# A new order for an attention turn, an identity matrix by VectorE, and tile addresses at multiples of 64 bytes, in a kernel of attention and two MLPs

## The chip, the cores and the metric

The kernel runs on one core of a Trainium2 chip. Its engines are TensorE (PE in the rows), VectorE (DVE), ScalarE (ACT), GpSimd (POOL) and SyncE (SP), which here issues nearly all loads and stores. Each engine works through its own queue in order and waits on semaphores for the others. The metric is the device time of one execution in microseconds (us), lower is better; the times given are medians of several runs.

## The reference

Linear attention with a feature map, then two MLPs, all in float32:

```python
def phi(x):                                   # q, k: (4, 8, 576, 64), w_phi: (64, 128)
    proj = np.einsum('bhsd,df->bhsf', x, w_phi)
    proj = proj - np.max(np.abs(proj), axis=-1, keepdims=True)
    return np.concatenate([np.exp(proj), np.exp(-proj)], axis=-1)
q_p, k_p = phi(q), phi(k)
kv = np.einsum('bhsf,bhsd->bhfd', k_p, v)
z = np.sum(k_p, axis=2)
x = np.einsum('bhsf,bhfd->bhsd', q_p, kv) / (np.einsum('bhsf,bhf->bhs', q_p, z)[..., None] + 1e-6)
x = x.transpose(0, 2, 1, 3).reshape(2304, 512)
h = x @ w1_in;  x = np.maximum(0.01 * h, h) @ w1_out          # w_in: (512, 2048), w_out: (2048, 512)
h = x @ w2_in;  out = (h * np.tanh(np.log1p(np.exp(h)))) @ w2_out   # h above 20: h itself
```

The MLP weights are random doubles; q, k, v and w_phi are float32.

## The kernel before

The 32 heads are worked in 16 pairs. A head has 576 positions: 512 main ones and 64 left over; the left-overs of two neighbouring pairs share a tile ("l" tiles, done every second turn). Products that need float32 accuracy are split in a high and a low half (`split`: ScalarE makes the high half, VectorE the low one) and done in three passes (`three`, L80 to L83). The products with kv and the second ones with q (`kv`, `nd`) are plain float32; each such matmul stands as two passes in the trace.

`attention(n)`, L435, is one turn. Three pairs are in work in it: t = n + 2 is loaded and transposed (`transposes`, L255, `q_left`, L282), p = n + 1 is projected (`q_proj` L316, `k_proj` L294, `k_proj_left` L304) and gets its exponentials of k (`k_exp` L402), w = n gets kv (L337) and the numerators and denominators (`nd` L355). The x of pair w - 1 is transposed into X (`x_t` L390). The order in which `attention` calls these is the order on every engine's queue: nothing reorders it later.

Some of what a turn does on the other engines: `q_proj` has ScalarE copy each of four pieces to qd, and after two of them GpSimd takes the maximum over partitions (`partition_all_reduce`, qm, L330; one for each head); `q_guard` (L333) subtracts it on VectorE. `k_guard` (L288) is a maximum and a subtraction on VectorE for each k projection. kv adds up in one PSUM bank, which ScalarE copies to the tile kv (L353); nd reads that tile. Banks come from two rings of four, "a" (projections, transposes) and "b" (kv, nd, x). The third `nd` of a pair (c == 2, the left-overs) keeps its bank as `lb` until `x_t` of the next turn has used it and VectorE has copied the result to X (L399).

Beside that the MLP weights, which come as pairs of 32-bit words of a double, are turned into float32: `Conv.step` (L121) takes one chunk of 128 x 512 in each turn from n = 1 on. VectorE clamps the high words (L147) and shifts the low ones (L149), ScalarE rebases (L150), VectorE puts sign and low bits together (e, L156) and, a turn later, joins them (c, L128); then the chunk is split (L166, L167) or stored to DRAM. `Conv.load` has SP load the next chunks into two `stage` buffers. After four of the turns, 8 to 11, `window` splits a part of X for the first MLP; turns 14 and 15 do the first two products of that MLP (`moe`) in place of transposes.

`load(i)` (L218) issues the loads of a pair on SP: kn, qn, for every second pair kl and ql, then the values vm and vl. The values have three buffers, so those of pair n + 3 go where those of pair n are. At the start `make_identity` (L194) has GpSimd build the identity that all transposes need; `start` (L407) works pairs 0 and 1 up to the first turn.

The functions that the diff touches, with their line numbers:

## Time and profile before

| what | value |
|---|---|
| median of 3 runs | 1033.09 us (1032.63 to 1036.21) |
| the profiled execution | 1029.51 us, span 1027.7 us |
| granted TensorE clock, mean | 0.999 |
| TensorE busy | 1001.1 us (97% of the span) |
| VectorE busy | 753.2 us (73%) |
| ScalarE busy | 501.3 us (49%) |
| GpSimd busy | 72.6 us (7%) |

A row of the timeline gives the start, the time, engine and line, operation, tiles (out<-in), shapes and count; in brackets the idle time of the engine before it and what ended that. Rows of one line that follow each other are put together, with their count behind an x. A row of the chain of waits gives the start, the time and the work that the end of the program hung on at that moment. The kernel's attention ends at about 241 us of the span; the rest is the two MLPs.

### The profile page before, as it was taken

To read this page: it belongs to the slowest core of one execution; us is meant where nothing else is said; L and a number is where in the kernel's file an instruction comes from. 1 tells how busy PE (TensorE), PEld (TensorE's weight loads), DVE (VectorE), ACT (ScalarE), POOL (GpSimd) and SP (SyncE) were. 2 spreads that over 40 slices of the span, in tenths; PEclk is the share of its full clock that TensorE was granted. 3 is DMA by queue.
4 is the path that set the end of the run, shared out by engine and by line. 5 is a ranking of instruction groups with operands and counts; after the bars stand their busy time and mean duration, and the time that the engine had idled before them with its cause. 6 is when DMAs were issued, how large, how long until landed. Compare 5 with 4: busy or idle time off the path is not lost.

```text
span 1027.7 us, 14556 instructions
## 1 busy us (share of the span) xinstructions
PE 1001.1 (97%) x5544; PEld 871.2 (85%) x5544; DVE 753.2 (73%) x1389; ACT 501.3 (49%) x839; POOL 72.6 (7%) x38
## 2 busy tenths in 40 slices
PE   6999999999999999999999999999999999999998
PEld 5999988998888888998888888888888988888886
DVE  5888898876995666666533546978876888868976
ACT  4666666654554333343333445545544555545543
POOL 3322333220000000000000000000000000000000
PEclk9999999999999999999999999999999999999999
DMA  4333323313541344444311221000100100001001
GB/s 130 111 111 111 100 82 93 121 43 113 160 148 42 123 144 154 134 144 136 110 62 31 93 82 62 1 1 0 41 1 1 41 1 21 1 1 41 1 1 42
DMA packets 55494, 72.84 MB, mean 71 GB/s; under 512 B 10496, under 2 KB 39808, under 8 KB 55424
## 3 DMA queue, kind: packets, MB, share of 16 engines
q1 hardware_dynamic: 55264, 71.84, 21.6%
q8 instruction: 44, 0.72, 0.3%
q14 instruction: 26, 0.21, 0.1%
q10 hardware_dynamic: 160, 0.07, 0.0%
HBM read 57.48 MB, written 14.42 MB: 70 GB/s over the span
## 4 chain that ended last, share of the span: by engine, by line
PE 92%; DVE 5%; issue 1%; ACT 1%; POOL 0%; ACTq 0%; DVEq 0%; POOLq 0%
PE a L81 14%; PE a L82 14%; PE a L83 14%; PE b L82 13%; PE b L81 13%; PE b L83 13%; PE b L373 6%; PE b L345 4%; DVE qd L335 1%; PE a L266 1%; DVE kd L291 1%; DVE mx L290 1%; ACT kv L353 1%; PE b L395 1%; PE b L350 1%
## 5 line engine op out<-in xcount | busy, mean ns | idle before, releaser
L81 PE MATMUL a<-wh,wh 128*128 128x512 f32 (+1 forms) x640 | 235.6, 368 | 0.0
L82 PE MATMUL a<-wl,wh 128*128 128x512 f32 (+1 forms) x640 | 235.4, 368 | 0.0
L83 PE MATMUL a<-wh,wl 128*128 128x512 f32 (+1 forms) x640 | 235.4, 368 | 0.0
L81 PEld LDWEIGHTS a<-wh,wh 128*128 128x128 f32 x640 | 120.6, 188 | 20.2
L82 PEld LDWEIGHTS a<-wl,wh 128*128 128x128 f32 x640 | 120.7, 189 | 20.1
L83 PEld LDWEIGHTS a<-wh,wl 128*128 128x128 f32 x640 | 120.6, 188 | 20.0
L571 DVE TENSOR_TENSOR gl<-g,gh 128x512 fp32r<-128x512 f32 x72 | 49.9, 693 | 110.1 <-ACT gh L568 110.1
L82 PE MATMUL b<-gl,wh 128*128 128x512 f32 (+1 forms) x320 | 117.7, 368 | 0.0
L81 PE MATMUL b<-gh,wh 128*128 128x512 f32 (+1 forms) x320 | 117.7, 368 | 0.0
L83 PE MATMUL b<-gh,wl 128*128 128x512 f32 (+1 forms) x320 | 117.7, 368 | 0.0
L82 PE MATMUL b<-wl,gh 128*128 128x512 f32 x288 | 112.1, 389 | 0.0
L81 PE MATMUL b<-wh,gh 128*128 128x512 f32 x288 | 112.1, 389 | 0.0
L83 PE MATMUL b<-wh,gl 128*128 128x512 f32 x288 | 112.1, 389 | 0.0
L568 ACT ACTIVATE gh<-g 128x512 fp32r<-128x512 f32 x72 | 45.5, 632 | 115.9 <-PE b L83 109.4
L330 POOL PARTITION_ALL_REDUCE qm<-qd x32 | 71.9, 2249 | 140.7 <-DVE qd L335 122.1
L593 ACT ACTIVATE gh<-u 128x512 fp32r<-128x512 f32 x72 | 45.6, 633 | 70.6 <-PE b L82 63.9
L567 DVE TENSOR_TENSOR g<-g,a 128x512 f32<-128x512 f32 x72 | 49.4, 686 | 38.0 <-ACT g L564 35.2
L150 ACT ACTIVATE c<-c 128x512 f32<-128x512 f32 x64 | 40.3, 630 | 68.5 <-DVE c L147 68.3
L373 PE MATMUL b<-kv,qp 128*128 128x65 f32 x512 | 62.7, 276 | 7.5 <-ACT kv L353 7.5
L620 ACT ACTIVATE r<-e,two 128x512 f32<-128x512 f32 x72 | 51.7, 718 | 36.3 <-DVE e L605 36.3
L83 PEld LDWEIGHTS b<-gh,wl 128*128 128x128 f32 x320 | 60.3, 189 | 10.1
L81 PEld LDWEIGHTS b<-gh,wh 128*128 128x128 f32 x320 | 60.4, 189 | 10.0
(103 smaller groups left out, 1773.7 us busy)
## 6 DMA issues: line engine op xcount, KB each, us to landing
stage<-in_moe_w_in_dram SPq DMA_DIRECT2D x32, 512.0 KB, 3.6
stage<-in_moe_w_out_dram SPq DMA_DIRECT2D x32, 512.0 KB, 3.5
scr<-c SPq DMA_DIRECT2D x37, 256.0 KB, 2.0
wstage<-scr SPq DMA_DIRECT2D x32, 256.0 KB, 3.8
kn<-in_k_dram SPq DMA_DIRECT2D x16, 256.0 KB, 3.8
qn<-in_q_dram SPq DMA_DIRECT2D x16, 256.0 KB, 4.0
vmain<-in_v_dram SPq DMA_DIRECT2D x16, 256.0 KB, 3.2
out_dram<-X SPq DMA_DIRECT2D x16, 256.0 KB, 2.2
```

Of the source, the lines that this page charges most:

```text
L81: nc.tensor.matmul(out=o, lhsT=wh_, rhs=xh, start=start, stop=False)
L82: nc.tensor.matmul(out=o, lhsT=wh_, rhs=xl, start=False, stop=False)
L83: nc.tensor.matmul(out=o, lhsT=wl_, rhs=xh, start=False, stop=stop)
L150: nc.scalar.activation(out=c, in_=c, func=AF.Copy, scale=2.0 ** -112)
L330: nc.gpsimd.partition_all_reduce(s["qm"][:, h, :], s["qd"][:, h, :], P, bass_isa.ReduceOp.absmax)
L345: nc.tensor.matmul(out=o, lhsT=s["kp"][a][:, h, t, :], rhs=s["vm"][:, h, t:NM + 1:NM - t, :], start=(c == 0 and t == 0), stop=False, skip_ ...
L373: nc.tensor.matmul(out=g[:, 2 * j + h, 0:D + 1], lhsT=s["qp"][a][:, h, Q_COL[h][u]:Q_COL[h][u] + P], rhs=s["kv"][:, 2 * h + a, 0:D + 1], s ...
L567: nc.vector.tensor_tensor(out=g, in0=g, in1=h, op=ALU.max)
L568: nc.scalar.activation(out=hi, in_=g, func=AF.Copy)
L571: nc.vector.tensor_tensor(out=lo, in0=g, in1=hi.bitcast(F32), op=ALU.subtract)
L593: nc.scalar.activation(out=hi2, in_=u2, func=AF.Copy)
L620: nc.scalar.activation(out=r0, in_=e0, func=AF.Ln, bias=two)
```

## The change

Four things:

1. The identity is built by VectorE out of a counted row, its transpose by 32 x 32 blocks and a comparison; GpSimd has no part in it any more.
2. The order of a turn is written anew. All four q projections, then the k projections, then kv by sign (each sign with its left-overs, and with the first sign's exponentials of the next pair between them), the copy of kv, the values' loads, q_guard for the *next* pair, the begin of a weight chunk, the transposes, the rebase, the second sign's exponentials, x of the pair before, and nd in two parts, with the join of the chunk between them. The left-overs of nd are in the second part and share its bank.
3. A chunk's work, `Conv.begin` and `Conv.join`, lies in one turn but for its low half. The loads of a pair's k and q stand at the head of the turn, those of its values behind kv.
4. Two tiles of 32 bytes stand in front of others, so that tiles start at multiples of 64 bytes. By the tile sizes, ident, wbd, the three vmain and two of the three vleft started 32 bytes off such a multiple before; all tiles behind them, but for the second buffers of mx and den, started at one. Now vleft1 alone of the larger ones is 32 bytes off.

```diff
+        def begin(self):
+            self.load(1)
+            if self.rest is not None:
+                self.rest()
+            self.rest = None
+            if self.at == len(self.units):
+                return lambda: None
+            u, kind = self.units[self.at]
+            self.at += 1
+            c = gp.tile([P, DM], F32, tag="c", name="c")
+            stg = self.stage.pop(u)
+            hw, lw = stg[:, :, 1], stg[:, :, 0]
+            nc.vector.tensor_scalar(out=c, in0=hw.bitcast(F32), scalar1=F64_TOP, scalar2=-F64_TOP,
+                                    op0=ALU.min, op1=ALU.max)
+            nc.vector.tensor_scalar(out=lw, in0=lw, scalar1=29, scalar2=None, op0=ALU.logical_shift_right)
+            self.open = (u, kind, c, hw, lw)
+            return lambda: nc.scalar.activation(out=c, in_=c, func=AF.Copy, scale=2.0 ** -112)
+        def join(self):
+            if self.open is None:
+                return
+            u, kind, c, hw, lw = self.open
+            self.open = None
+            e = gp.tile([P, DM], I32, tag="w1", name="e", bufs=1)
+            nc.vector.scalar_tensor_tensor(out=e, in0=hw, scalar=-(1 << 31), in1=lw,
+                                           op0=ALU.bitwise_and, op1=ALU.bitwise_or)
+            self.load(1)
+            nc.vector.scalar_tensor_tensor(out=c.bitcast(I32), in0=c.bitcast(I32), scalar=3, in1=e,
+                                           op0=ALU.logical_shift_left, op1=ALU.bitwise_or)
+            if kind == "store":
+                scr[self.which, u] = dr.tile([P, DM], F32, name=f"scr{self.which}_{u}")
+                nc.sync.dma_start(out=scr[self.which, u], in_=c)
+            else:
+                self.rest = split_w(self.which, u // 2, u % 2, c)
...
+    def identity(out):
+        Q = 32
+        one, row, col = (ap.tile([P, Q], F32, name=x, bufs=1) for x in ("one", "row", "col"))
+        nc.vector.memset(one, 1.0)
+        nc.vector.memset(out, 0.0)
+        nc.vector.tensor_tensor_scan(out=row, data0=one, data1=one, initial=0.0, op0=ALU.mult, op1=ALU.add)
+        nc.vector.transpose(out=col, in_=row)
+        for r in range(0, P, Q):
+            nc.vector.tensor_tensor(out=out[r:r + Q, r:r + Q], in0=row[r:r + Q], in1=col[r:r + Q], op=ALU.is_equal)
...
-        ident = ap.tile([P, P], F32, name="ident", bufs=1)
-        make_identity(nc, ident)
+        pad = [ap.tile([P, 8], F32, name="pad0", bufs=1)]
         wbd = ap.tile([P, 2, F], F32, name="wbd", bufs=1)
         nc.vector.memset(wbd, 0.0)
+        ident = ap.tile([P, P], F32, name="ident", bufs=1)
+        identity(ident)
...
+        pad.append(ap.tile([P, 8], F32, name="pad1", bufs=1))
...
+            def values():
+                vm = s["vm"] = vmain[i % NV]
+                nc.sync.dma_start(
+                    out=vm[:, :, 0:NM, :].rearrange("p h t d -> p h (t d)"),
+                    in_=v[b, h0:h0 + 2, 0:MAIN, :].rearrange("h (p t) d -> p h (t d)", t=NM),
+                )
+                vl = s["vl"] = vleft[i % NV]
+                for r in range(2):
+                    nc.sync.dma_start(out=vl[r * LEFT:(r + 1) * LEFT, r, 0:D], in_=v[b, h0 + r, MAIN:S, :])
+            return values
...
+        def kv(i, a):
             s, l = st[i], lf[i // 2]
-            h, a = divmod(c, 2)
-            if c == 0:
+            if a == 0:
                 s["kvp"] = bank("b")
-            o = s["kvp"][:, c * P:(c + 1) * P]
-            for t in range(NM):
-                nc.tensor.matmul(out=o, lhsT=s["kp"][a][:, h, t, :], rhs=s["vm"][:, h, t:NM + 1:NM - t, :],
-                                 start=(c == 0 and t == 0), stop=False, skip_group_check=True)
-            if c == 3:
-                both = s["kvp"].rearrange("p (h a n) -> p h a n", h=2, a=2)
-                for x in range(2):
-                    nc.tensor.matmul(out=both[:, :, x, 0:D + 1], lhsT=l["lp"][x][:, i % 2, :], rhs=s["vl"],
-                                     start=False, stop=(x == 1), skip_group_check=True)
-                s["kv"] = ap.tile([P, 4, P], F32, tag="kv", name="kv", bufs=1)
-                nc.scalar.activation(out=s["kv"], in_=s["kvp"].rearrange("p (c n) -> p c n", n=P), func=AF.Copy)
+            both = s["kvp"].rearrange("p (h a n) -> p h a n", h=2, a=2)
+            for h in range(2):
+                for t in range(NM):
+                    nc.tensor.matmul(out=both[:, h, a, :], lhsT=s["kp"][a][:, h, t, :], rhs=s["vm"][:, h, t:NM + 1:NM - t, :],
+                                     start=(a == 0 and h == 0 and t == 0), stop=False, skip_group_check=True)
+            nc.tensor.matmul(out=both[:, :, a, 0:D + 1], lhsT=l["lp"][a][:, i % 2, :], rhs=s["vl"],
+                             start=False, stop=(a == 1), skip_group_check=True)
+        def kv_copy(i):
+            s = st[i]
+            s["kv"] = ap.tile([P, 4, P], F32, tag="kv", name="kv", bufs=1)
+            nc.scalar.activation(out=s["kv"], in_=s["kvp"].rearrange("p (c n) -> p c n", n=P), func=AF.Copy)
...
+            ng = 4 + 2 * c
+            g = t[:, 0:ng * (D + 1)].rearrange("p (c n) -> p c n", n=D + 1)
...
+            if c == 1:
                 kv_ = s["kv"].rearrange("p (h a) n -> p h a n", a=2)
                 for a in range(2):
-                    nc.tensor.matmul(out=g, lhsT=s["qp"][a].rearrange("p h n -> p (h n)")[:, MAIN:MAIN + P], rhs=kv_[:, :, a, 0:D + 1],
-                                     start=(a == 0), stop=(a == 1))
-                ng = 2
-            else:
-                g = t.rearrange("p (c n) -> p c n", n=P)
-                for j, u in enumerate(range(2 * c, 2 * c + 2)):
-                    for h in range(2):
-                        for a in range(2):
-                            nc.tensor.matmul(out=g[:, 2 * j + h, 0:D + 1], lhsT=s["qp"][a][:, h, Q_COL[h][u]:Q_COL[h][u] + P],
-                                             rhs=s["kv"][:, 2 * h + a, 0:D + 1], start=(a == 0), stop=(a == 1))
-                ng = 4
-            den = ap.tile([P, 4], F32, tag="den", name="den")[:, 0:ng]
+                    nc.tensor.matmul(out=g[:, 4:6], lhsT=s["qp"][a].rearrange("p h n -> p (h n)")[:, MAIN:MAIN + P],
+                                     rhs=kv_[:, :, a, 0:D + 1], start=(a == 0), stop=(a == 1))
...
+            o = s["lb"][:, MAIN - LEFT:MAIN]
...
+        def k_exp(i, a):
+            sg = 1 - 2 * a
             if i % 2 == 0:
-                lf[i // 2]["lp"] = [exp(lf[i // 2]["kd"], "lp", sg) for sg in (1, -1)]
-            st[i]["kp"] = [exp(st[i]["kd"], "kp", sg) for sg in (1, -1)]
+                lf[i // 2].setdefault("lp", []).append(exp(lf[i // 2]["kd"], "lp", sg))
+            st[i].setdefault("kp", []).append(exp(st[i]["kd"], "kp", sg))
...
+            kp_head(1, 0)
             transposes(1, "k")
             lf[0]["lp"] = [exp(lf[0]["kd"], "lp", sg) for sg in (1, -1)]
             transposes(1, "q")
             q_left(1)
-            kp_head(1, 0)
+            kp_head(0, 1)
             kp_head(1, 1)
+            q_guard(0)
             kv(0, 0)
-            kv(0, 1)
-            load(2)
+            load(2)()
...
         def attention(n):
             t, p, w = n + 2, n + 1, n
             has_t, has_p, has_w = t < PAIRS, 0 <= p < PAIRS, 0 <= w < PAIRS
-            def q_exp(sg):
-                if sg == 1:
-                    st[w]["qp"] = []
-                st[w]["qp"].append(exp(st[w]["qd"], "qp", sg))
+            values = load(t + 1) if t + 1 < PAIRS else lambda: None
+            if has_p:
+                for c in range(4):
+                    q_proj(p, c)
             if has_w:
-                q_guard(w)
+                st[w]["qp"] = [exp(st[w]["qd"], "qp", sg) for sg in (1, -1)]
             if has_p:
-                q_proj(p, 0)
-                k_proj(p, 0)
-                q_proj(p, 1)
+                for c in range(2):
+                    k_proj(p, c)
+                if p % 2 == 0:
+                    k_proj_left(p)
             if has_w:
                 if w:
                     kv(w, 0)
-                q_exp(1)
+                if has_p:
+                    k_exp(p, 0)
+                kv(w, 1)
+                kv_copy(w)
+            values()
             if has_p:
-                q_proj(p, 2)
-                k_proj(p, 1)
-            if has_w:
-                q_exp(-1)
-            if has_p:
-                q_proj(p, 3)
-                if p % 2 == 0:
-                    k_proj_left(p)
-            if n >= CONV0 and not conv0.done():
-                conv0.step()
-            if has_w:
-                for c in range(1 if w else 2, 4):
-                    kv(w, c)
+                q_guard(p)
+            rebase = conv0.begin() if n >= CONV0 else lambda: None
             if has_t:
                 transposes(t)
                 q_left(t)
             elif has_w:
                 moe(n - (PAIRS - 2))
+            rebase()
             if has_p:
-                k_exp(p)
-            if has_w:
-                nd(w, 0)
+                k_exp(p, 1)
             if 0 <= w - 1:
                 x_t(w - 1)
             if has_w:
+                nd(w, 0)
+            conv0.join()
+            if has_w:
                 nd(w, 1)
-                nd(w, 2)
-            if t + 1 < PAIRS:
-                load(t + 1)
```

How the change moves instructions on three queues. **SP**, the loads of turns 0 and 1 (kn, qn, kl, ql, vmain and vleft are a pair's loads, stage a chunk's), before:

```order
L239 DMA vmain0_88<-in_v_dram 128x2x256
L245 DMA vleft0_91<-in_v_dram 64x64 x2
L115 DMA stage_468<-in_moe_w_in_dram 128x4x256
L115 DMA stage_470<-in_moe_w_out_dram 128x1024
L115 DMA stage_478<-in_moe_w_in_dram 128x4x256
L224 DMA kn_567<-in_k_dram 128x2x256
```

and with the change:

```order
L298 DMA vleft0_99<-in_v_dram 64x64 x2
L275 DMA kn_411<-in_k_dram 128x2x256
L275 DMA qn_413<-in_q_dram 128x2x256
L285 DMA kl_415<-in_k_dram 64x2x64 x2
L285 DMA ql_418<-in_q_dram 64x2x64 x2
L292 DMA vmain1_97<-in_v_dram 128x2x256
L298 DMA vleft1_100<-in_v_dram 64x64 x2
L114 DMA stage_507<-in_moe_w_in_dram 128x4x256
L114 DMA stage_509<-in_moe_w_out_dram 128x1024
```

The first two chunks stood right behind the values of pair 3 (vmain0); now the whole of pair 4 stands between, with its values (vmain1), which overwrite those of pair 1.

**ScalarE**, the part of turn 2 around the copy of kv (wh is a weight chunk's high half, c its rebase, kth, qth, lh the transposes' high halves, kp the exponentials of k), before:

```order
L166 ACTIVATE wh_636<-c 128x512
L150 ACTIVATE c<-c 128x512
L353 ACTIVATE kv<-b 128x512
L77 ACTIVATE kth<-a 128x512
L77 ACTIVATE qth<-a 128x2x256
L77 ACTIVATE lh<-a 128x256
L313 ACTIVATE kp<-kd 128x1024 x2
L396 ACTIVATE X<-b 128x512
```

and with the change:

```order
L368 ACTIVATE kp<-kd 128x1024
L409 ACTIVATE kv<-b 128x512
L76 ACTIVATE kth<-a 128x512
L76 ACTIVATE qth<-a 128x2x256
L76 ACTIVATE lh<-a 128x256
L137 ACTIVATE c<-c 128x512
L368 ACTIVATE kp<-kd 128x1024
L449 ACTIVATE X<-b 128x512
L202 ACTIVATE wh_566<-c 128x512
```

The rebase c has gone from in front of the copy of kv to behind the transposes' halves; in front of it now stands one kp; the weight split is the turn's last.

**VectorE**, the middle of turn 2 (ktl, qtl, ll are the transposes' low halves, den the denominators; before, q_guard, qd<-qd,qm, is five rows ahead of this piece, at the head of the turn), before:

```order
L128 SCALAR_TENSOR_TENSOR c<-c,e 128x512
L147 TENSOR_SCALAR c<-stage 128x512
L149 TENSOR_SCALAR stage<-stage 128x512
L167 TENSOR_TENSOR wl_637<-c,wh_636 128x512
L156 SCALAR_TENSOR_TENSOR e<-stage 128x512
L78 TENSOR_TENSOR ktl<-a,kth 128x512
L78 TENSOR_TENSOR qtl<-a,qth 128x2x256
L78 TENSOR_TENSOR ll<-a,lh 128x256
L286 CAST qth<-lh 128x64
L286 CAST qtl<-ll 128x64
L377 TENSOR_SCALAR den<-b 128x4
L378 RECIPROCAL den<-den 128x4
```

and with the change:

```order
L390 TENSOR_TENSOR qd<-qd,qm 128x1152
L203 TENSOR_TENSOR wl_567<-c,wh_566 128x512
L133 TENSOR_SCALAR c<-stage 128x512
L135 TENSOR_SCALAR stage<-stage 128x512
L77 TENSOR_TENSOR ktl<-a,kth 128x512
L77 TENSOR_TENSOR qtl<-a,qth 128x2x256
L77 TENSOR_TENSOR ll<-a,lh 128x256
L341 CAST qth<-lh 128x64
L341 CAST qtl<-ll 128x64
L452 COPY X<-b 128x64
L431 TENSOR_SCALAR den<-b 128x4
L432 RECIPROCAL den<-den 128x4
```

q_guard stands in the middle of the turn, in front of the chunk's clamp and of the transposes' halves; e and the join c have gone behind the first nd, and the copy that frees the bank lb (X<-b) stands in front of that nd's denominators.

## Rows read from the trace of the kernel before

**Rows 1.** The page, part 1: busy time, share, instructions of each engine.
```profile
PE 1001.1 (97%) x5544; PEld 871.2 (85%) x5544; DVE 753.2 (73%) x1389; ACT 501.3 (49%) x839; POOL 72.6 (7%) x38
```

**Rows 2.** The waits of TensorE: for whom, us in total, times, longest.
```profile
PE a L266 <- POOL ident masks.py:199: 9.2, 1, 9.2
PE b L373 <- ACT kv L353: 7.5, 12, 1.2
```

**Rows 3.** The timeline of TensorE: the first q projection of turns 2 and 14.
```profile
43.58 0.39 PE L81 MATMUL a<-qth,wbh 128*128 128x320 f32 x1
...
213.19 0.39 PE L81 MATMUL a<-qth,wbh 128*128 128x320 f32 x1
```

**Rows 4.** The chain of waits, 66 to 100 us: start, us, what.
```profile
71.67 0.15 PE a L81
...
72.11 0.12 PE a L81
...
75.61 2.68 PE b L345 x24
...
78.73 0.87 PE a L266 x8
...
79.83 0.58 ACT kv L353
...
80.46 2.00 PE b L373 x16
...
83.07 1.80 PE b L373 x16
```

**Rows 5.** The timeline of VectorE and GpSimd in the same turn.
```profile
72.96 1.36 DVE L335 TENSOR_TENSOR qd<-qd,qm 128x1152 f32<-128x1152 f32 x1
74.35 0.69 DVE L290 TENSOR_REDUCE mx<-a 128x4 f32<-128x512 f32 x1
...
77.07 0.68 DVE L128 SCALAR_TENSOR_TENSOR c<-c,e 128x512 int32<-128x512 int32 x1
77.67 1.52 DVE L147 TENSOR_SCALAR c<-stage 128x512 f32<-128x512 f32 x1
...
74.48 2.14 POOL L330 PARTITION_ALL_REDUCE qm<-qd  x1 [9.26 <-DVE qd L335]
77.32 2.62 POOL L330 PARTITION_ALL_REDUCE qm<-qd  x1 [0.69 <-ACT qd L328]
```

**Rows 6.** The tile stage up to 245 us: ns min/median/max; its loads to landing.
```profile
L147 DVE TENSOR_SCALAR c<-stage x15: 420/1030/1522, 36.3 to 231.0; 128x512 f32<-128x512 f32 x15
L149 DVE TENSOR_SCALAR stage<-stage x15: 410/1101/1105, 37.3 to 231.4; 128x512 int32<-128x512 int32 x15
...
DMA to landing us min/median/max: 3.4/3.6/5.0
```

**Rows 7.** The timeline of the start, 0 to 20 us.
```profile
3.31 1.25 SPq L234 DMA_DIRECT2D ql<-in_q_dram  x2
...
8.86 0.28 POOL masks.py:199 TENSOR_SCALAR_AFFINE_SELECT ident<-ident 128x128 f32<-128x128 f32 x1 [7.93 <-issue]
...
11.24 0.56 PE L81 MATMUL a<-wbh,kth 128*128 128x256 f32 x1
...
15.03 4.30 POOL L330 PARTITION_ALL_REDUCE qm<-qd  x2 [5.89 <-ACT qd L328]
...
19.52 0.39 PE L81 MATMUL a<-qth,wbh 128*128 128x320 f32 x1 [0.70 <-DVE qtl L286]
```

**Rows 8.** The tile ql up to 20 us: its loads, from issue to landing.
```profile
DMA to landing us min/median/max: 2.0/2.1/2.2
```

**Rows 9.** The timeline of SP's queue, 20 to 30 us: values, then the first chunk.
```profile
24.62 0.37 SPq L239 DMA_DIRECT2D vmain<-in_v_dram  x1
...
26.24 0.58 SPq L115 DMA_DIRECT2D stage<-in_moe_w_in_dram  x1
```

**Rows 10.** The page, part 5: an activation's last operation in the first MLP.
```profile
L571 DVE TENSOR_TENSOR gl<-g,gh 128x512 fp32r<-128x512 f32 x72 | 49.9, 693 | 110.1 <-ACT gh L568 110.1
```

More of the change, by code (lines that the diff above doesn't have):

```diff
@@ L9 @@
 from concourse._compat import with_exitstack
-from concourse.masks import make_identity
 F32 = mybir.dt.float32
@@ L97, in __init__ @@
             self.which, self.units, self.at, self.loaded = which, units, 0, 0
-            self.stage, self.open = {}, None
+            self.stage, self.open, self.rest = {}, None, None
         def load(self, ahead):
@@ L237, in load @@
                         )
-            vm = s["vm"] = vmain[i % NV]
-            nc.sync.dma_start(
-                out=vm[:, :, 0:NM, :].rearrange("p h t d -> p h (t d)"),
-                in_=v[b, h0:h0 + 2, 0:MAIN, :].rearrange("h (p t) d -> p h (t d)", t=NM),
-            )
-            vl = s["vl"] = vleft[i % NV]
-            for r in range(2):
-                nc.sync.dma_start(out=vl[r * LEFT:(r + 1) * LEFT, r, 0:D], in_=v[b, h0 + r, MAIN:S, :])
+            def values():
[8 more added lines that the diff above has]
+            return values
         for r in range(2):
             nc.scalar.dma_start(out=wbd[r * D:(r + 1) * D, r, :], in_=w_phi)
-        load(0)
-        load(1)
+        load(0)()
+        load(1)()
         wbh = ap.tile([P, 2 * F], F32R, name="wbh", bufs=1)
@@ L419, in start @@
             kp_head(0, 0)
-            kp_head(0, 1)
             k_proj(0, 1)
```

22 lines of the change are left out of this document (11 added, 11 removed).

## The prediction

> **What bounds the kernel now.** First the busy shares of the page: TensorE is busy 97% of the span [rows 1], so only its gaps and its order can be shortened; the two MLPs behind the attention keep it busy without a gap. Then its waits: 9.2 us once for the identity at the start, and 7.5 us in 12 waits for the copy of kv by ScalarE [rows 2]. The reader is to see that these lie in the attention, the first quarter of the span. There the unit is one turn, from the first q projection to the next turn's: turns 2 to 13 run from 43.58 to 213.19 us, 12 turns of 14.13 us on the mean [rows 3].
>
> The chain of waits through one turn gives the price of each piece of TensorE's work [rows 4]. A pass of a projection costs 0.15 us at 320 columns and 0.12 at 256; 24 passes of kv 2.68 us, so 0.112 each; 8 transposes 0.87; 16 passes of nd 1.80 us, but 2.00 behind a wait; the transposes of x with the fold, from the end of the first nd at 80.46 + 2.00 = 82.46 to the second at 83.07, 0.61 us. A turn without any wait is then: q projection 6 x 0.15 + 6 x 0.12 = 1.62; k projection 12 x 0.12 = 1.44; kv and its left-overs, 36 passes, 4.03; transposes 0.87; x 0.61; nd 2 x 1.80 and its left-overs 0.45; in all 12.6, and about 0.3 for the left-overs of q and k that each pair of turns does once. That is **12.9 us, against 14.13 now**: 1.2 us of a turn are waits and the refilling behind them.
>
> Why does kv wait? The copy of kv begins at 79.83, although TensorE is through with kv at 78.73 [rows 4]: ScalarE's queue has the rebase of a weight chunk ahead of it, and that waits for VectorE's clamp, which took 1.52 us at 77.67, beside an all-reduce of GpSimd from 77.32 on [rows 5]. The clamp takes 0.42 us at best [rows 6].
>
> **The change part by part.** The profiled execution took 1029.51 us for a span of 1027.7; the median of the three runs is 1033.09, 3.6 us above. I make the sum against the profiled one and carry the difference over to the median.
>
> *Identity by VectorE: 4.7 us earlier.* Today the identity comes at 8.86 + 0.28 = 9.14 us, after 7.93 us in which GpSimd waits for nothing that the profile shows [rows 7]. Eight VectorE instructions on 32 or 128 columns replace it. The trace shows no scan and no transpose of VectorE; from above they are bounded by 0.69 us each, the price of 512 columns [rows 5], which would end near 6.6 us, from below by almost nothing, which would end near 1.1. With a quarter or less of the columns I take 0.3 each, so 3.5 us. The next thing late is a load anyway: the second part of ql is issued at about 3.31 + 0.63 = 3.94 [rows 7] and lands 2.1 us later [rows 8], at 6.05; its transpose stands ahead of the first k projection. That starts at 11.24 now [rows 7] and can start at about 6.4. Everything behind it in the start moves by up to 4.9 us; I take 4.7, because TensorE's first matmuls were slow (0.56 us for one of 256 columns at 11.24 [rows 7], against 0.39 for one of 320 at 43.58 [rows 3]) and waits among them may stretch that. Bounds: 3.5 and 5.1. Turn 0 then begins at 14.8 and not at 19.52 [rows 7].
>
> *The order of a turn on ScalarE: the kv wait goes.* The rebase now stands behind the splits of the transposes. With the turn's first q projection as zero, TensorE comes to q, k to 3.1, kv of both signs to 7.1, transposes to 8.0 (8.2 with left-overs), x to 8.7, the first nd to 10.5, the second to 12.8. The copy of kv can run at 7.3 to 7.9 and is needed at 8.7. What is late next? VectorE: q_guard now waits for both all-reduces within the same turn. They begin with the copy of the second q piece, at about 1.65, and take 2.14 us each (the pair at the start 4.30 [rows 7]): 5.95. VectorE's k_guards end at 5.35, its left-overs at 6.15: 77.07 - 74.35 = 2.72 us for two chunks [rows 5], from 2.6 on. Then q_guard 1.39 (74.35 - 72.96 [rows 5]), the low half of the weight chunk 0.6, clamp and shift 0.35 + 0.45, two splits of 0.61, the casts, and only then the copy that frees the bank in which the second nd must write. I get 10.75 us in turns with left-over transposes, 10.6 in the others; TensorE asks for it at 10.5 to 10.7. So a wait of about 0.35 us, refilling included, in every second turn: **13.1 us a turn** and 12 x (14.13 - 13.08) = 12.6 us over turns 2 to 13. The clamp no longer meets an all-reduce, since q_guard stands ahead of it; that is why I use 0.35 to 0.45 and not 1.52.
>
> *The first weight chunk: 4.8 us lost, once.* In turn 1 the first load of a chunk now stands on SP's queue behind the values of pair 4, which go to the buffer that kv of this very turn reads: not before 7.3. Before, the load was issued 1.62 us after the previous values [rows 9], ahead of this turn; it lands 3.6 us later, at most 5.0 [rows 6]. 7.3 + 1.6 + 4.0 = 12.9, where VectorE's clamp is due at 7.5. All that stands behind the clamp on VectorE moves, the bank's copy to 15.4: the second nd waits 4.7 us. TensorE refills slowly behind a long idle time; bounds 0 and 1.7, I take 0.9. Turn 0 also takes 11.1 us, since its copy of kv stands behind kp, and that behind k_guard. From 19.52 to 43.58 turns 0 and 1 took 24.1 us [rows 3, 7]; now 11.1 + 12.9 + 5.6 = 29.6, so 5.5 more.
>
> *The last turns: 1.9 us lost.* In turns 14 and 15 the MLP's first activations, four operations of some 0.69 us [rows 10] in turn on two engines, stand on VectorE ahead of the copy that frees the bank: 0.8 us twice. The join of the last chunk puts some 0.3 us ahead of the last x.
>
> *Alignment: nothing.* By the sizes of the tiles only the identity, wbd, vmain and two of the three vleft lay 32 bytes off a multiple of 64. kv reads vmain and pays 0.112 us a pass; nd reads the tile kv, at a multiple already, and pays 1.80 / 16 = 0.112 [rows 4]. Bounds: 1 ns on 32 passes in 16 turns, half a microsecond either way. Fewer VectorE instructions in nd (a denominator and its reciprocal less) lie under the waits above.
>
> Sum: -4.7 + 5.5 - 12.6 + 1.9 = **-9.9 us**: 1019.6 for an execution like the profiled one, 1023.2 for the median.
>
> A rule that would change the start: the Trainium skill, "GPSIMD Engine Reference", section on instruction dispatch, says that the first call to freshly loaded code pays a load of some 6 us. By it the new first use of GpSimd, the all-reduce, would pay it and not the identity. This is a rival below.
>
> **Rivals.**
> *A, GpSimd's code load moves to the all-reduce.* If the load waits until the operands are there, at 15.03 - 4.7 - 0.4 = 9.95, and takes the 5.9 us that GpSimd stood idle ahead of 15.03 (up to the 7.9 of the first [rows 7]), the first all-reduce starts at 15.85, later than now, and the start gives back about 4: 1027. For it: the 7.93 us are a fixed price somewhere. Against it: the first all-reduce ran at 15.03, released by ScalarE's copy [rows 7], 5.9 us after another code was in use, so the load went on in the background; the new one has from 0.93 to 9.95. Chance 0.08. The Trainium skill's rule read strictly gives this time; the row speaks for a load ahead of the call.
>
> *B, better: the first chunk lands early and the bank is free in time.* Then turns run at 12.9 and turn 1 loses 1 or 2 us: -16, so 1017. Chance 0.14.
>
> *C, VectorE's chain is longer by half a microsecond or one.* Every operation added between q_guard and the bank's copy delays the second nd one to one. With 0.8 us more in each turn 9.6 of the 12.6 are given back: 1033. For it: the chain has a dozen operations and each wait for a semaphore counts. Chance 0.10.
>
> *D, slower: the all-reduce closes a loop.* ScalarE's weight split waits for VectorE's join, the q copies stand behind it, the all-reduces behind those, then q_guard and the chain up to the next join. With the prices above that loop is 0.7 to the weight split, 1.4 to the second q copy, 4.3 for the all-reduces, 1.4 for q_guard, 0.6 + 0.8 for the weight chunk, 1.2 for two splits, 0.8 for the third, the casts and the copy, 1.35 for the first nd's operations and the join's first: 12.6 us, just under TensorE's 12.9. It decides from 12.9 on; from 13.9 on all that the start gains and the first chunk costs is no longer paid for, and from 14.3 on the kernel is slower by over 0.5%. With the longest rows (all-reduces of 2.62 [rows 5], clamp and shift at 1.52 and 1.10 [rows 6]) it is 15.4, and 12 turns cost 15 more instead of 12.6 less: 1051. Against it: what made those rows long is the meeting of all-reduce and clamp, which the new order excludes; and a k_guard at 74.35 beside an all-reduce from 74.48 on kept its 0.69 us [rows 5]. Chance 0.08.
>
> **How the numbers follow.** Forecast 0.60, A 0.08, B 0.14, C 0.10, D 0.08. The forecast's own range is 1018 to 1028: start 1.2 and first chunk with its refilling 2 either way, 0.2 us in each of 12 turns. With the lower side of B and with C the range is 1014 to 1033. A measurement of this kernel can tell 0.5% from no change, about 5.2 us: faster is below 1027.9. Faster: 0.56 of the forecast, B, half of A: 0.74. Same: C, the other half, 0.04 of the forecast: 0.18. Slower: D, 0.08.
>
> **What would show it.** Right: the first transposes at 3.5 to 4.5 us, the first k projection at 6 to 7; no wait of nd for kv in turns 2 to 13; these turns near 13.1 us; one wait of 4 to 5 us in turn 1, released by VectorE, with a clamp that waits for a load; small waits of nd for VectorE's copy to X; the clamp at 0.4 us. Wrong: turns of 14 us (C or D), the first all-reduce later than 11 us (A), no long wait in turn 1 (B), or matmuls of kv at another pace than 0.112 (alignment).

## The result, and the profile after

The changed kernel takes **1016.43 us** (median of 5 runs, 1014.7 to 1017.49) against 1033.09 us before: a ratio of 0.9839, with a 95% interval of 0.9815 to 0.9864, so 16.7 us less. That lies in the predicted range (1014 to 1033), on its fast side; the forecast was 1023.2. The profiled execution of after took 1016.43 us as well, for a span of 1014.5: 13.1 us less than that of before (1029.51). The other 3.6 us are what before's profiled execution lies under its median. In the runs made for the experiments, executions of before with a mean granted clock of 0.999 or 1.000 took 1029.3 to 1030.5 us, those at 0.996 or 0.997 1031.8 to 1033.2, and one at 0.555, which stands in no ratio, 1703, so a single execution tells two or three us only with its clock beside it.

Page of after, part 1, and TensorE's waits in after (for whom, us in total, times, longest); they answer to [rows 1, 2]:

```profile
PE 1000.7 (99%) x5544; PEld 873.7 (86%) x5544; DVE 732.6 (72%) x1365; ACT 500.4 (49%) x839; POOL 68.7 (7%) x36
```

```profile
PE a L321 <- DMA kn<-in_k_dram: 3.6, 1, 3.6
PE a L80 <- DVE qtl L341: 2.7, 2, 2.1
PE a L80 <- ACT qd L383: 1.1, 1, 1.1
PE b L448 <- DVE xn L433: 0.9, 1, 0.9
PE b L422 <- ACT kv L409: 0.7, 1, 0.7
PE a L331 <- DMA ql<-in_q_dram: 0.4, 1, 0.4
```

The 9.2 us for the identity have become 3.6 for a load, and of the waits for the copy of kv one of 0.7 us is left, in turn 0. New are 2.1 us for qtl and 1.1 for qd, both at the head of turn 2 (the other wait for qtl, 0.6 us, is the one ahead of turn 0). No row names VectorE's copy to X, for which the forecast had waits in every second turn.

The timeline of TensorE in after, the first q projection of turns 0 to 3 and 14, and behind it that of turn 3 before (the others of before are in [rows 3, 7]):

```profile
14.30 0.39 PE L80 MATMUL a<-qth,wbh 128*128 128x320 f32 x1 [0.63 <-DVE qtl L341]
...
25.43 0.39 PE L80 MATMUL a<-qth,wbh 128*128 128x320 f32 x1
...
40.73 0.38 PE L80 MATMUL a<-qth,wbh 128*128 128x320 f32 x1 [2.09 <-DVE qtl L341]
...
57.48 0.39 PE L80 MATMUL a<-qth,wbh 128*128 128x320 f32 x1
...
199.96 0.39 PE L80 MATMUL a<-qth,wbh 128*128 128x320 f32 x1
```

```profile
57.20 0.39 PE L81 MATMUL a<-qth,wbh 128*128 128x320 f32 x1
```

These rows and the spans make the balance, in us:

| stretch | before | after | difference | forecast |
|---|---|---|---|---|
| up to turn 0 | 19.52 | 14.30 | -5.2 | -4.7 |
| turns 0 to 2 | 37.68 | 43.18 | +5.5 | +4.4 (5.5 for turns 0 and 1, -1.05 for turn 2) |
| turns 3 to 13 | 155.99 | 142.48 | -13.5 | -11.6 |
| turn 14 to the end of the span | 814.5 | 814.5 | 0.0 | +1.9 |
| sum | 1027.7 | 1014.5 | -13.2 | -9.9 |

Turns 3 to 13 take 142.48 / 11 = 12.95 us, the floor that the prediction had worked out from TensorE's own passes (12.9), and not the 13.08 of the forecast.

One such turn in after, the one that begins at 83.27, from the timelines of ScalarE, VectorE and TensorE:

```profile
91.02 0.60 ACT L409 ACTIVATE kv<-b 128x512 f32<-128x512 f32 x1
...
92.46 0.64 ACT L137 ACTIVATE c<-c 128x512 f32<-128x512 f32 x1
...
91.24 0.42 DVE L133 TENSOR_SCALAR c<-stage 128x512 f32<-128x512 f32 x1
...
93.54 0.22 DVE L452 COPY X<-b 128x64 f32<-128x64 f32 x1
...
92.24 3.74 PE L422 MATMUL b<-kv,qp 128*128 128x65 f32 x32
```

The copy of kv (L409) runs at 91.02, in front of the rebase (L137, 92.46), and is through 0.6 us before nd (L422) starts; nd's 32 passes run on without a gap. In [rows 4, 5] the copy stood behind the rebase and the rebase behind a clamp of 1.52 us. The clamp takes 0.42 us now, in all turns, as the tile stage in after shows (ns min/median/max; [rows 6] before):

```profile
L133 DVE TENSOR_SCALAR c<-stage x15: 418/420/428, 38.5 to 216.3; 128x512 f32<-128x512 f32 x15
L135 DVE TENSOR_SCALAR stage<-stage x15: 418/423/425, 38.9 to 216.6; 128x512 int32<-128x512 int32 x15
```

The start of after, from the timelines of VectorE, TensorE, ScalarE and GpSimd:

```profile
1.21 0.20 DVE L233 TENSOR_TENSOR_SCAN row<-one 128x32 f32<-128x32 f32 x1
1.45 0.21 DVE L234 STREAM_TRANSPOSE col<-row 128x32 f32<-128x32 f32 x1
1.70 0.77 DVE L236 TENSOR_TENSOR ident<-row,col 32x32 f32<-32x32 f32 x4
...
6.23 0.45 PE L331 MATMUL a<-ident,ql 128*128 128x128 f32 x1 [0.38 <-DMA ql<-in_q_dram]
6.33 0.56 PE L80 MATMUL a<-wbh,kth 128*128 128x256 f32 x1
...
8.59 0.74 ACT L383 ACTIVATE qd<-a 128x320 f32<-128x320 f32 x2 [1.49 <-PE a L82]
...
9.42 4.26 POOL L385 PARTITION_ALL_REDUCE qm<-qd  x2 [8.99 <-ACT qd L383]
```

The identity is there at 2.47 us, ahead of the loads; the first k projection starts at 6.33 (11.24 before, [rows 7]), and the first all-reduce 0.09 us behind the copy that feeds it.

Turn 1 and the head of turn 2 in after, from the timelines of SP's queue, VectorE and TensorE:

```profile
34.54 0.58 SPq L114 DMA_DIRECT2D stage<-in_moe_w_in_dram  x1
...
38.53 0.43 DVE L133 TENSOR_SCALAR c<-stage 128x512 f32<-128x512 f32 x1 [5.63 <-DMA stage<-in_moe_w_in_dram]
...
40.60 0.22 DVE L452 COPY X<-b 128x64 f32<-128x64 f32 x1
...
35.74 2.40 PE L422 MATMUL b<-kv,qp 128*128 128x65 f32 x20
37.98 0.66 PE L428 MATMUL b<-kv,qp 128*128 128x130 f32 x4
```

The late first chunk is there as forecast: issued at 34.54 (26.24 before, [rows 9]), and VectorE's clamp waits 5.63 us for it. But TensorE runs through its second nd (the x20 are the last 20 of the 32 passes of both) up to 38.6, two us before the copy to X on which the forecast let it wait. It stops only at the next turn, for qtl (40.73), then for the q copies. Behind these stops its granted clock falls, as the windows of after show (us, busy us of TensorE, granted clock, DMA share):

```profile
39.00:42.00 3.00, 1.27 (x10) 1.00 0.01 4
42.00:45.00 3.00, 1.85 (x9) 0.51 0.55 165
45.00:48.00 3.00, 3.00 (x17) 0.50 0.54 188
48.00:51.00 3.00, 3.00 (x24) 0.85 0.00 0
51.00:54.00 3.00, 3.00 (x30) 1.00 0.29 89
```

At 0.50, the lower of its two levels (1.2 GHz), 17 passes fit in 3 us where 30 fit later. Turn 1 took 15.30 us and turn 2 16.75 in place of some 12.95; the forecast had 18.5 and 13.1.

### The profile page after: what moved, and what is told of

Read it like the earlier page. It is cut to its first block, busy times and chain, and to the rows that moved or that the text cites. A ratio compares the mean times of both kernels' runs of the same rounds, so it can differ in the third digit from the quotient of the medians.

```text
span 1014.5 us, 14523 instructions
## 1 busy us (share of the span) xinstructions
PE 1000.7 (99%) x5544; PEld 873.7 (86%) x5544; DVE 732.6 (72%) x1365; ACT 500.4 (49%) x839; POOL 68.7 (7%) x36
## 4 chain that ended last, share of the span: by engine, by line
PE 97%; DVE 1%; DMA 1%; SPq 0%; ACT 0%; issue 0%; DVEq 0%; ACTq 0%
PE a L80 15%; PE a L81 15%; PE a L82 15%; PE b L80 13%; PE b L81 13%; PE b L82 13%; PE b L401 6%; PE b L422 5%; PE a L321 1%; PE b L428 1%; PE b L403 1%; PE b L448 1%; DMA stage<-in_moe_w_in_dram 0%; PE b L451 0%; DMA ql<-in_q_dram 0%
## 5 line engine op out<-in xcount | busy, mean ns | idle before, releaser
L385 POOL PARTITION_ALL_REDUCE qm<-qd x32 | 68.5, 2188 | 136.9 <-ACT qd L383 136.9
L81 PEld LDWEIGHTS b<-gl,wh 128*128 128x128 f32 x320 | 60.3, 189 | 10.0
L634 ACT ACTIVATE e<-a 128x512 f32<-128x512 f32 x72 | 43.0, 597 | 47.7 <-PE a L82 27.0
```

Of the source, the lines that this page charges most:

```text
L81: nc.tensor.matmul(out=o, lhsT=wh_, rhs=xl, start=False, stop=False)
L385: nc.gpsimd.partition_all_reduce(s["qm"][:, h, :], s["qd"][:, h, :], P, bass_isa.ReduceOp.absmax)
L634: nc.scalar.activation(out=e0, in_=h0, func=AF.Exp)
```

## Experiments

Three questions: is the gain that of the two edits that the forecast named (identity, rebase)? Why did nd not wait for the bank? And what do the late first chunk, q_guard's place and the alignment cost or bring? Each run is compared with runs of the kernel before on the same chip (medians 1031.8 us beside e1 to e4, 1032.09 beside e5 to e8, 1032.57 beside e9).

| kernel | us | ratio to before, 95% |
|---|---|---|
| the change | 1016.43 | 0.9839 (0.9815 to 0.9864) |
| e1, identity alone | 1026.13 | 0.9954 (0.9938 to 0.9971) |
| e5, rebase alone | 1021.01 | 0.9900 (0.9885 to 0.9915) |
| e9, both of these | 1015.25 | 0.9831 (0.9806 to 0.9856) |
| e2, change without pads | 1016.10 | 0.9849 (0.9834 to 0.9864) |
| e3, fold on nd's columns | 1016.39 | 0.9857 (0.9837 to 0.9877) |
| e8, second nd in bank lb | 1020.71 | 0.9896 (0.9878 to 0.9914) |
| e7, rebase first again | 1029.06 | 0.9976 (0.9965 to 0.9987) |
| e6, q_guard at the head | 1014.91 | 0.9844 (0.9828 to 0.9860) |
| e4, first chunks early | 1011.75 | 0.9810 (0.9794 to 0.9826) |

**e1, the identity alone.** Against before:

```diff
-        make_identity(nc, ident)
         wbd = ap.tile([P, 2, F], F32, name="wbd", bufs=1)
         nc.vector.memset(wbd, 0.0)
+        identity(ident)
```

> The kernel before with the identity built by VectorE, and nothing else of the change. Theory: the start and the order of a turn are separate gains that add up. Turn 0's first q projection came at 14.30 us after the change and at 19.52 before, so this kernel should begin turn 0 near 14.5 us and keep that head start through turns of the old length (14.1 us): 1033.1 - 5.2 = 1027.9 us, with 1026.5 to 1029.5 allowed. Rival: the old order can't use the earlier start, because in turns 0 and 1 something else (the first weight chunk, issued at 26.2 us before) ends later than TensorE; then the head start shrinks by turn 3 and the time is 1030 to 1033 us.

Measured: 1026.13 against 1031.8, -5.7 us by the medians, 4.8 (3.0 to 6.4) by the ratio. The time itself is 0.4 us under the range given, because before was faster there too (1031.8 against 1033.09); the difference is as expected. Turn 0 begins at 14.79, turn 2 at 38.84 and turn 14 at 208.45 us, each 4.7 earlier than before [rows 3, 7]. The head start goes through the old order whole.

**e5, the rebase alone**, and **e9, both.** e5 against before (e9 is e5 with the edit of e1):

```diff
-                    nc.scalar.activation(out=c, in_=c, func=AF.Copy, scale=2.0 ** -112)
+                    f = lambda c=c: nc.scalar.activation(out=c, in_=c, func=AF.Copy, scale=2.0 ** -112)
+                    if late:
+                        self.late = f
+                    else:
+                        f()
...
-                conv0.step()
+                conv0.step(late=True)
...
             elif has_w:
                 moe(n - (PAIRS - 2))
+            if conv0.late is not None:
+                conv0.late()
+                conv0.late = None
```

> The kernel before with one thing moved: ScalarE's rebase of a weight chunk stands behind the splits of the transposes, and so behind the copy of kv, as in the change; identity, q_guard and all else stay. Theory: the wait for the copy of kv (7.5 us in 12 waits, and the slower first passes of nd behind each, some 0.2) is what the rebase in front costs, and goes: 12 x 0.83, so 8 to 10 us, a ratio of 0.990 to 0.992, and turns near 13.4 us where 14.13 stood. Rival: the clamp of 1.0 to 1.5 us beside an all-reduce, and VectorE behind it, hold the turn as well, so the wait only moves to another name (VectorE's kd, qtl or den) and less than 3 us are won.

> The kernel before with the two single edits together: identity by VectorE, and the rebase behind the transposes' splits; q_guard, kv, nd, the weight chunk's loads and the tile addresses stay as before. Alone they gave -4.8 us (ratio 0.9954 of 1031.8) and -10.3 us (0.990 of 1032.1). Theory: they add up, -15 to -16 us, 1016 to 1017.5, so these two lines give as much as the whole change did (0.984), and the rest of the new order nets nothing: it gains some 0.37 us in each turn with a chunk (13.26 on the mean with the rebase alone, 12.89 after the change) and gives 6 back where the first chunk comes late. Rival: the earlier start runs into the first chunk or into the loads of pair 2 once turns are shorter, or the two gains share a wait: 1019 or more. Second rival: the rest of the order is worth something beside the first chunk's loss: the two edits alone stay at 1018 to 1020 and the change is faster than they are.

Measured: e5 1021.01 us, a ratio of 0.990 (-10.3 us); turns 2 to 13 run from 44.16 to 204.90, 13.40 each where 14.13 stood. In its waits the copy of kv is gone and short ones are left:

```profile
PE a L81 <- DVE kd L295: 1.7, 3, 0.7
PE b L369 <- DVE X L403: 0.8, 2, 0.6
```

e9: 1015.25 us, ratio 0.9831, -17.3 by the medians; that is 0.75 us under the range given, with a gain of 15 to 16 expected (by the ratio's interval it is 14.9 to 20.0). The two gains add up within the noise, and these two edits do all that the whole change does. What then is the rest of the new order worth? e9's turns 3 to 13 take (199.09 - 51.43) / 11 = 13.42 us, those of the change 12.95. In e9 TensorE waits for VectorE in both kinds of turn. In one (13.07 to 13.61 us, 12.82 to 13.02 in the change) the chain of waits (start, us, what) runs along VectorE:

```profile
66.40 1.36 DVE qd L350
...
70.60 0.60 DVE c L128
71.20 1.44 DVE c L147
72.64 1.02 DVE stage L149
...
77.36 0.14 DVE X L414
77.50 0.00 issue
77.50 0.68 PE b L380 x4
```

The clamp and the shift still meet an all-reduce (1.44 and 1.02 us), and at the end of VectorE's row TensorE's third nd (L380) waits. The profile names the copy to X (L414) as its releaser, but by the program's list of instructions it waits for the operation just ahead of that, the division xn (L401), which is the last to read the first nd's bank; the third nd gets that bank, and the copy to X frees another one. In the other kind of turn (13.44 to 13.97 us, 12.96 to 13.17 in the change) the projection of k's left-overs waits for VectorE's k_guard, from 0.1 us up to this row of TensorE's timeline:

```profile
135.81 0.35 PE L81 MATMUL a<-wbh,lh 128*128 128x256 f32 x1 [0.67 <-DVE kd L306]
```

So the rest of the new order takes 0.47 us from each of these 11 turns, 5.2 in all, and gives 6.1 back in turns 0 to 2, where e9 needs 51.43 - 14.31 = 37.12 us and the change 43.18. The 43.18 us of the change hold the late first chunk and the clock behind it: the span of e4 (below), without them, is 1008.2 us and that of e9 1013.3, so the rest of the order is worth some 5 us once the chunk is early. Both rivals of e9's expectation fall.

**e2, no pads.** Against the change:

```diff
-        pad = [ap.tile([P, 8], F32, name="pad0", bufs=1)]
...
-        pad.append(ap.tile([P, 8], F32, name="pad1", bufs=1))
```

> The changed kernel without the two small tiles in front of others; every tile behind them is where the old layout rule puts it, so some lie 32 bytes off a multiple of 64. Theory: alignment is worth nothing: 16 passes of kv keep 1.78 us (0.111 each), 1016.4 us, within 1.5 either way. Rival: the alignment is part of the gain that the forecast did not see: the passes that read vmain or vleft take longer, by 5% (0.09 us for 16 passes, 2 x 16 turns: 2.8 us), and the time is 1019 us or more.

Measured: 1016.10 us, and 16 passes of kv in 1.78 us as with the pads; the rows of the chain of waits in e2 and then in after:

```profile
85.54 1.78 PE b L399 x16
```

```profile
86.90 1.78 PE b L401 x16
```

The alignment of these tiles brings nothing here. Of others e2 says nothing: by the built programs' addresses the pads move ident, wbd, vmain and two of the three vleft to multiples of 64, while the chunk's tiles (stage, c, wh, wl) and the MLPs' weight tiles start 32 bytes off one in before, in the change and in e2 alike.

**e3, the fold on nd's columns, and e8, the bank lb.** Both against the change:

```diff
 e3:
-            o = s["lb"][:, MAIN - LEFT:MAIN]
+            o = s["lb"][:, 0:LEFT]
 e8:
                 nd(w, 1)
+                nc.vector.tensor_copy(out=held, in_=st[w]["kvp"][:, 0:1])
```

> The changed kernel with the fold's result put at the front of the bank lb, on columns that the second nd writes, and no longer at its end, which no matmul of nd writes. Theory: the forecast's wait of the second nd for VectorE's copy to X was absent because the columns don't meet; where they meet, the wait exists. In turn 1 that copy ended at 40.82 us while TensorE came to the second nd at 36.2, so a wait of some 4.6 us appears there, of which the later waits of turn 2 (2.1 for qtl, 1.2 for the q copies) give back most: 1 to 3 us net. In the ordinary turns the copy ended at 10.49 us of the turn and TensorE came at 10.61, so nothing or little; the last two turns, where four activations stand ahead of the copy, 0.8 us each. In all 1018 to 1021 us. Rival: the place in the bank has no part in it, and the copy is simply early enough: 1016.4 us and turns as before, without any wait of nd for VectorE. Second rival: the copy is just late in half of the turns, as forecast: 0.35 us in each second turn on top, 1021 to 1024.

Measured: 1016.39 us and no wait of nd for VectorE. My theory of the columns fell: the copy to X read nd's columns at 41.53 us, while the second nd had been through since 39.6, so the two can't be in one bank at all. The program's list of instructions says it (second nd of turn 1; in the program of the change b_569 lies in the bank of b_478, which is kv of this turn, and b_394 is lb, which VectorE copies to X):

```
change  L422 MATMUL b_569<-kv_501,qp_445 128x65 [waits PE_49]
change  L452 COPY X_75<-b_394 128x64 [waits PE_49]
e8      L423 MATMUL b_571<-kv_503,qp_447 128x65 [waits DVE_49]
```

The ring of four is no strict rotation. In the change the second nd has the bank of its own turn's kv in every turn from 1 on; that bank is free, since ScalarE's copy of kv reads it last. The bank that the copy to X frees goes to the next turn's kv, which comes later. A late reader of kv's bank keeps it taken, and then the second nd gets lb's and has to wait for VectorE (DVE): that is e8.

> The changed kernel with one small VectorE copy behind each turn's second nd, that reads one column of kv's bank (nothing uses its result). It keeps that bank taken until there, so that the second nd gets the bank lb of the turn before, as the forecast had it, in place of the bank that the copy of kv has freed. Theory: the forecast's terms for the bank were right in kind and only did not apply: in turn 1 the second nd waits from 36.2 to 40.9 us for VectorE's copy to X, of which the later waits of turn 2 (2.1 and 1.2 us) give back part, 1.5 to 3.5 net; in the ordinary turns the copy ends at 10.49 us and TensorE comes at 10.61, so 0 to 0.1 us each; in the last two turns 0.5 to 0.8 each. In all 3 to 6 us more than the changed kernel: 1019 to 1022.5. Rival: the bank is not what the forecast missed; the second nd doesn't wait even so, and the time is 1016.4 within 1.5.

Measured: 1020.71 us, 4.3 over the change. All waits of nd for VectorE's copy to X, timeline of TensorE in e8:

```profile
40.98 1.33 PE L423 MATMUL b<-kv,qp 128*128 128x65 f32 x5 [4.40 <-DVE X L453]
...
161.72 2.00 PE L423 MATMUL b<-kv,qp 128*128 128x65 f32 x16 [0.26 <-DVE X L453]
...
216.08 2.00 PE L423 MATMUL b<-kv,qp 128*128 128x65 f32 x16 [0.54 <-DVE X L453]
...
228.31 2.00 PE L423 MATMUL b<-kv,qp 128*128 128x65 f32 x16 [0.54 <-DVE X L453]
```

With lb's bank the forecast's waits exist: 4.40 us in turn 1 (forecast 4.7), 0.54 twice in the last turns with 0.2 of slow passes each behind them (forecast 0.8 twice). In the ordinary turns the list has one of 0.26 us and no other: the copy is early enough there, by 0.1 to 0.3 us. The parts, too, are as expected: against the change's trace turn 1 is 4.3 us longer, turn 2 2.1 shorter, turns 3 to 13 0.7 longer and the last turns 1.2. The granted clock is 0.50 to 0.54 from 39 to 48 us here too.

**e7, the rebase in front of the copy of kv again.** Against the change:

```diff
-                kv_copy(w)
             values()
...
             rebase = conv0.begin() if n >= CONV0 else lambda: None
+            rebase()
+            if has_w:
+                kv_copy(w)
...
-            rebase()
```

> The changed kernel with the copy of kv put behind VectorE's begin of the chunk and ScalarE's rebase, in that order, as they stood before the change. Theory: nd waits for kv again in each turn with a chunk. In turn 7 kv was through at 116.54 us and the clamp at 117.44; the rebase would end near 118.0 and the copy near 118.7, where nd began at 118.02: 0.7 us of wait and 0.2 to 0.3 of slow passes behind it, in some 14 turns: 13 us, 1027 to 1031. Rival: with the clamp no longer beside an all-reduce the copy is late by so little that nd hardly notices: under 4 us, 1020 at most.

Measured: 1029.06 us, +12.6 on the change, its gain nearly gone. Waits of TensorE in e7:

```profile
PE b L422 <- ACT kv L409: 10.9, 11, 5.5
```

The sum was as expected, its parts were not quite. The turns behind turn 2 wait 0.40 to 0.86 us each, most of them under 0.5, and turns 3 to 13 take 7.3 us more than in the change; the other 5.1 us arise in turns 1 and 2, since now the copy of kv, too, waits for the late first chunk (the 5.5 us of the row), and the granted clock behind that wait is 0.50 from 39 to 51 us.

**e6, q_guard at the head of the turn.** Against the change:

```diff
+            if has_w:
+                q_guard(w)
             if has_p:
                 for c in range(4):
                     q_proj(p, c)
...
-            if has_p:
-                q_guard(p)
             rebase = conv0.begin() if n >= CONV0 else lambda: None
```

> The changed kernel with q_guard moved back to the head of the turn, for the pair w, where it stood before; all else as changed. Theory: the turn is at TensorE's own 12.9 us because ScalarE's copy of kv has nothing in front of it; q_guard's place has no part in that. VectorE then comes to the clamp some 0.4 us after the all-reduces are through (head 1.35 + 1.36, k_guards 2.7, the low half 0.6 make 6.3 us of the turn, against 5.9), so the clamp stays at 0.42 us: 1016.4, within 2 us. Rival: the clamp meets an all-reduce again in some turns (1.0 to 1.5 us in the rows), the exponentials of q come later by up to 1.4 us on ScalarE, and turns rise to 13.3 us or more: 1021 or more.

Measured: 1014.91 us, turns of 12.82 and 12.96 in turn: no effect on the time, as the theory had it. Its reason was wrong, though, as the tile stage in e6 shows:

```profile
L133 DVE TENSOR_SCALAR c<-stage x15: 416/633/1179, 38.6 to 215.8; 128x512 f32<-128x512 f32 x15
```

The clamp does meet an all-reduce again (median 0.63 us, up to 1.18). It costs nothing here: what stands behind it on VectorE still comes before TensorE wants it, and the turns stay at the floor.

**e4, the first chunks early.** Against the change:

```diff
             load(2)()
+            conv0.load(1)
```

> The changed kernel with the loads of the first two weight chunks issued in the start, behind the values of pair 2, and not in turn 1 behind those of pair 4. Theory: turns 1 and 2 took 15.30 and 16.75 us only because VectorE's first clamp waited 5.6 us for its chunk and TensorE's clock fell behind that wait; with the chunk there they take 12.9 to 13.2 each, the granted clock stays at 1.0 from 38 to 50 us, and the time is 1016.4 - 6 = 1010.4 us, 1009 to 1012. Rival: the two early loads of 512 KB each collide with the loads of pairs 2 and 3, which then come late: transposes wait for kn or qn in turn 0 or 1, and less than half is won, 1013.5 us or more. Second rival: the slow turn 2 has another cause (the first all-reduces, or the weight split that stands ahead of the q copies), so turn 2 stays above 15 us and the time near 1014.

Measured: 1011.75 us (1010.43 to 1013.45), 4.4 and 4.6 less than e2 and e3 on the same chip, and the fastest of all kernels here. Turns 1 and 2 take 12.96 and 12.82 us. The windows of e4 show no gap and no fall of the clock where after has both:

```profile
39.00:42.00 3.00, 3.00 (x27) 1.00 1.01 316
42.00:45.00 3.00, 3.00 (x29) 1.00 0.08 28
45.00:48.00 3.00, 3.00 (x30) 1.00 0.34 96
```

So the first chunk's late load is all that made those turns long, and the two loads, issued at 15.02 and 15.65 us, collide with nothing that is waited for. The theory holds; both rivals fall. e4 beats the kernel before by 1.9% and the change by some 0.4%.

## Why the prediction was right, and which of its steps were not

- **Identity by VectorE**: -4.7 forecast, -5.2 in the change's trace and 4.7 at turn 0 in e1. Scan and transpose took 0.20 and 0.21 us, under the 0.3 assumed, and as forecast the loads were late next (ql at 6.2, the first k projection at 6.33). Where the start is the same the head start still varies, from 4.3 us (e3, turn 0 at 15.24) to 5.3 (e7, 14.23): in e3 passes of 256 columns stand 0.21 us apart up to 10.2 us, in after up to 7.8.
- **The order on ScalarE**: the mechanism was right and carries the larger part: the rebase alone gives 10.3 us (e5), and put back in front it takes 12.6 (e7). That the clamp drops to 0.42 us was right too, but as a cause in the new order it is worth nothing (e6).
- **The bank lb, the step that failed**: "only then the copy that frees the bank in which the second nd must write". The second nd writes in the bank of its own turn's kv. So the 0.35 us in every second turn and the 1.9 us of the last turns were not there, and turns ran at the floor of 12.95. Where e8 gives nd that bank, turn 1 and the last turns wait about as priced (4.40 and 0.54 with 0.2 behind it), and of the waits only the ordinary turns' 0.35 was too much. e8's profiled execution took 1021.02 us, the sum had 1019.6; that they are so near is in part chance, since turns 0 to 2 take 45.43 us there, 7.8 more than before where the sum had 4.4.
- **The first weight chunk**: +5.5 for turns 0 and 1, of which turn 2's 1.05 is to be taken off; measured +5.5 for turns 0 to 2, of which only 2.4 lie in turns 0 and 1. The place on SP's queue and the clamp's wait were right, the way to TensorE was not: not the second nd, but qtl and the q copies, 2.09 and 1.15 us, and then the clock. Of the 0.9 us for "refilling" no row of before gives the size. What follows the stop in the profiled execution is the lower clock, and it costs more: turn 2 took 16.75 us there, and 14.50 in e2's, where the granted clock stayed at 1.00 behind waits as long.
- **Alignment**: nothing, as forecast (e2).
- **The sum against the median**: 3.6 us were carried over from before's profiled execution to its median. After's profiled execution is its median, so of the 6.8 us between the forecast of 1023.2 and the result 3.6 are this step and 3.2 the terms above. The same holds for the gain: of the 16.7 us by the medians 13.1 stand in the two traces; executions at 0.999 or 1.000 differ by some 15 us (1014.7 in after, 1029.3 to 1030.5 in before).
- **The rivals**: A is out: the first all-reduce started 0.09 us after its operands. By the rule of the Trainium skill ("GPSIMD Engine Reference", instruction dispatch) the first call would have paid some 6 us; the trace doesn't show it on the call. C and D did not occur: VectorE had time to spare (busy 10.6 and 10.9 us in two ordinary turns of 12.82 and 12.96). The result stands nearer to B's 1017 than to the forecast, and B is right in half: turns at the floor, and no wait of 4 to 5 us in turn 1, but the first chunk late. That the median comes out at B's time is luck: the two traces differ by 13.1 us, where B had 16. e4 is B whole, and its gain by the ratio, 19.6 us, is above the 16 given for B.

What stays open: in which part of an execution of before the clock falls where its mean is 0.996, since no such execution of it was profiled (a fall doesn't need the late chunk: one of e4's four executions has 0.996 and took 1013.45 us, the others 1010.43 to 1012.34); and which of the remaining moves (kv by sign, nd in two parts, the join behind the first nd) takes the 0.47 us off an ordinary turn, since they were not run one by one.

## What to carry to other kernels

In a queue that works in order, ask of each short copy that the busiest engine waits for what stands ahead of it and what that in turn waits for: here one operation of 0.64 us, moved behind work that was ready, gave 10 of 17 us, and a new order of everything else gave nothing net until the first chunk's load was put right. When a step moves behind another on a load queue, look at its first use and not at the steady turns: one load that came 8 us later cost 4 to 6 us, and a line that issues it early gave them back. And before a wait for a buffer goes into a sum, read from the built program which buffer a tile really gets, and what a wait is for; the profile names the work that ended last.

## What the runs showed of the hardware that was not expected

- **The clock falls behind a short stop, but not each time.** In after TensorE's rows show 1.27 us of work in 39 to 42, and the granted clock is 0.51 and 0.50 in 42 to 48; passes of a k projection then stand 0.21 us apart instead of 0.12, and 16 passes of kv take 2.79 us instead of 1.78. In e3, e6, e7 and e8 the clock falls in this stretch as well. In e2 it has 0.79 us of work in 39 to 42 and 1.58 in 42 to 45, and the clock stays at 1.00; its turn 2 is 2.25 us shorter:

```profile
39.00:42.00 3.00, 0.79 (x7) 1.00 0.26 107
42.00:45.00 3.00, 1.58 (x13) 1.00 0.19 53
```

  The column alone doesn't tell all: at the start of e2 it reads 1.00 from 6 to 9 us, where passes of 256 columns stand 0.21 us apart; from 9.9 on they stand 0.12 apart.
- **Beside an all-reduce VectorE's clamp takes longer, but is not held until the all-reduce is through.** In [rows 5] the clamp begins 0.35 us into an all-reduce of 2.62 us and ends 0.75 us before it, 1.52 us long where 0.42 is its price alone; the all-reduce is listed with 2.62 us where 2.14 is its usual time. Whether the clamp runs slowly or stands still for a part of it the trace doesn't show. The Trainium skill ("SBUF — State Buffer", "Who interferes with whom") says that of a VectorE instruction in a two-port mode and one of GpSimd the later is blocked until the other is through. If the clamp is such an instruction, that does not hold here for a whole all-reduce as the trace lists it.
